# Linear attention and a channel mixer on one core: first half of k requested before lam, first transposes ahead of lam's product, powers of lam after the first mask product

## The chip, the cores and the metric

The kernel runs on 1 core of one Trainium2 chip. The time is device microseconds (us) of that core for one launch. Engines are TensorE (PE; its weight loads are PEld), VectorE (DVE), ScalarE (ACT), GpSimd (POOL) and SyncE (SP). Each takes its instructions in the order in which they stand in its queue. SP and ACT also issue the DMAs here.

## The reference

Inputs q, k, v are (batch 4, heads 8, sequence 768, width 64), lam has one decay per head. The attention is worked in blocks with a running state; its output becomes x, of shape (4, 768, 512), and a mixer follows.

```python
Dmask = np.where(rel >= 0, lam ** rel, 0.0)          # rel = i - j inside a block
intra = (qb @ kb.T * Dmask) @ vb
inter = (qb * lam ** (pos + 1)) @ kv_state
out[block] = intra + inter
kv_state = lam ** block * kv_state + (kb * lam ** (block - 1 - pos)).T @ vb
...
u = x + (x.T @ U @ V).T                              # per batch
result = u + np.maximum(u @ w_ch1, 0) @ w_ch2
```

## The kernel before, in words

The sequence is cut into tiles of 128 positions, 6 per batch, 24 in all; a tile is called s. For a tile, `prep` transposes q and k on TensorE (eight heads, two per transpose, so four transposes each, written to PSUM as `pq` and `pk`) and ScalarE copies them to `qt` and `kt` (L351). `scores` multiplies them into `pss` (L393); `masked` multiplies `pss` by the decay mask on VectorE into `sm` (L402); `intra` multiplies `sm` with v into `px` (L446). `inter` adds `qs` times the running state to the same `px` (L434); `qs` is `qt` times the powers `powq`, made on GpSimd in `scale` (L376). `state` makes the next state `kv` from `ks` (k times `rev`, GpSimd, L365) and v (L411). The first tile of a batch has no state, so tile 0 needs no `qs`; tile 1 is the first that does.

All of the attention part is in an order written out by hand: `manual_schedule` is entered, the opening is written as plain calls, and then the list `pieces` is run from its first entry to its last. The list's order is the order in each engine's queue. After `intra(s)` come `state(s)`, `scores(s+1)`, `inter(s+1)`, `masked(s+1)`, `fade(s+1)`, and `prep(s+2)` stands ahead of `intra(s+1)`.

The opening makes what the tiles need. `lam` (eight numbers) is loaded into `lam_row`, spread over 128 partitions by a small TensorE product `pl` (L662), and copied to `lamb` (L664). From it VectorE makes the mask by eight scans (L302, in `constants`) and the powers `powq` by a memset, two copies and four scans (L308 to L314, in `powers`). `rev` is a column of the mask (L667). `scale_k(0)` then makes tile 0's `ks`.

`keep_busy(n)` issues n products of a zero tile `blank` on TensorE (L336), whose result nobody reads. In PSUM they stand in the buffer that `pq` uses.

Tile 0 is loaded in two halves of four heads each for q and k (`parts(0)` is 2), so that `turn_half(0, 0, ...)` can transpose the first half before the second has landed. The q halves are asked for on SP's DMA queue, the k halves on ACT's; all later loads are on SP's:

```python
nc.scalar.dma_start(out=lam_row[:, 0:H], in_=lam.unsqueeze(0))
load_next("q", nc.sync)
load_next("k", nc.scalar)
```

From 122 us on the mixer's two products (L714, L724, then L847 to L851) fill the rest of the time on TensorE.

In this trace one dummy product shows as two instructions.

Of the kernel before, what the change touches and what calls it, by code (L numbers as in the profile page):

```python
# [14 lines left out]
P = 128  # L15
# [3 lines left out]
def kernel(  # L19
# [28 lines left out]
    nc = tc.nc  # L48

    B, H, S, D = q.shape  # L50
    HP = H // 2
    NT = S // P
    C = H * D
# [34 lines left out]
    def set_ends(t):  # L88
        nc.vector.memset(t[:, 0:1], 1151.0)
        nc.vector.memset(t[:, 1:2], 255.0 * (1 << 23))  # L90
        ends.append(t)
# [153 lines left out]
    def two_banks(name, tag):  # L245
        return psf.tile([P, 2, N], FP32, tag=tag, name=name)

    def one_bank(shape, name, tag):
        return psf.tile(shape, FP32, tag=tag, name=name)
# [11 lines left out]
    def parts(s):  # L261
        return 2 if s == 0 else 1

    def load(name, s, engine):
        b, c = divmod(s, NT)
        t = raw_pool.tile(
            [P, H, D], FP32, tag=f"{name}raw", bufs=4 if name == "k" else 3, name=f"{name}raw"
        )
        source = {"q": q, "k": k, "v": v}[name]
        n = H if name == "v" else H // parts(s)  # L270
        for h in range(0, H, n):
            engine.dma_start(
                out=t[:, h : h + n, :],
                in_=source[b, h : h + n, c * P : (c + 1) * P, :].rearrange("h p d -> p h d"),
            )
        raw[s, name] = t
# [21 lines left out]
    def constants():  # L298
        for a in range(HP):
            for x in range(2):  # L300
                h = 2 * a + x
                nc.vector.tensor_tensor_scan(  # L302
                    mask[:, x, a, :], lamb[:, h : h + 1].broadcast_to([P, P]), ident, 0.0,
                    ALU.mult, ALU.add,
                )

    def powers():
        nc.vector.memset(zeros, 0.0)  # L308
        for x in range(2):
            nc.vector.tensor_copy(  # L310
                out=lamh[x * D : (x + 1) * D, :], in_=lamb[x * D : (x + 1) * D, x::2]
            )
        for a in range(HP):
            nc.vector.tensor_tensor_scan(  # L314
                powq[:, a, :], lamh[:, a : a + 1].broadcast_to([P, P]),
                zeros.broadcast_to([P, P]), 1.0, ALU.mult, ALU.add,
            )
# [13 lines left out]

    def keep_busy(n):

        out = one_bank([P, C], "idle", "pq")
        for i in range(n):
            nc.tensor.matmul(out=out[:, 0:P], lhsT=blank, rhs=blank, start=True, stop=True)  # L336

    qts, kts = {}, {}

    def turn_half(s, a0, name):  # L340

        ts, tag = (qts, ("pq", "pt")) if name == "q" else (kts, ("pk", "pu"))
        if a0 == 0:
            ts[s] = att.tile([P, HP, P], FP32, tag=name + "t", bufs=2, name=name + "t")
        n = HP // parts(s)
        pt = one_bank([P, n, P], "p" + name, tag[a0 > 0])
        for a in range(a0, a0 + n):
            nc.tensor.transpose(  # L348
                out=pt[:, a - a0, :], in_=raw[s, name][:, 2 * a : 2 * a + 2, :], identity=ident
            )  # L350
        nc.scalar.copy(ts[s][:, a0 : a0 + n, :], pt)  # L351

    def prep(s):
        for a0 in range(0, HP, HP // parts(s)):
            for name in "qk":
                turn_half(s, a0, name)
        st[s].update(qt=qts.pop(s), kt=kts.pop(s))
        for name in "qk":
            load_next(name)
# [144 lines left out]
    uhl, ud, turned = {}, {}, {}  # L504
# [39 lines left out]


    pieces = [("prep", 0), ("scale", 0), ("scores", 0), ("inter", 0), ("masked", 0)]
    for s in range(NS):
        b, c = divmod(s, NT)
        done = s - NT - 1
        more = s + 1 < NS  # L550
        step = [("prep", s + 1), ("scale", s + 1)] * more
        step += [("mix", done)] * (0 <= done < NS - NT - 1)
        step += [("low", b - 1)] * (c == 0 and b > 0)
        step += [("low_rows", b - 1)] * (c == 0 and b > 0)
        step += [("intra", s)]
        step += [("next_of_low", b - 1)] * (c == 0 and b > 0)
        step += [("late", s)] * (done < 0) + [("state", s)]
        step += [("next_of_low", b - 1)] * (c == 0 and b > 0)
        step += [("turned", done - 1)] * (done > 0) + [("late", s)] * (done >= 0)
        step += [("next_of_low", b - 1)] * (c == 0 and b > 0)  # L560
        step += [("scores", s + 1)] * more
        step += [("aside", s)] * (done >= 0)
        step += [("inter", s + 1), ("masked", s + 1), ("fade", s + 1)] * more
        step += [("aside", s)] * (done < 0)
        step += [("turn", done)] * (done >= 0 and done // TG < FG)
        pieces += step
    waiting = {name: list(range(NS)) for name in "qkv"}

    def load_next(name, engine=nc.sync):
        if waiting[name]:  # L570
            load(name, waiting[name].pop(0), engine)


    run = {
        "prep": prep, "fade": fade, "scores": scores, "masked": masked, "inter": inter,
        "intra": intra, "state": state,
        "low": low, "low_rows": low_rows, "next_of_low": next_of_low, "mix": mix, "turn": turn,
        "scale": scale, "turned": lambda s: turned.pop(s)(),
    }
    def v_steps():  # L580

# [64 lines left out]
    lam_row = consts.tile([1, H + P], FP32, name="lam_row")  # L646
    blank = x_pool.tile([P, C], FP32, tag="x", name="blank")[:, 0:P]
    nc.vector.memset(blank, 0.0)
    nc.vector.memset(lam_row[:, H:], 1.0)
    set_ends(vp[:, S + C : S + C + 2].bitcast(FP32))  # L650
    nc.scalar.dma_start(out=lam_row[:, 0:H], in_=lam.unsqueeze(0))
    load_next("q", nc.sync)
    load_next("k", nc.scalar)
    for name in "qkvkv":
        load_next(name)
    aside(-1)
    for name in "qkv":
        load_next(name)
    make_identity(nc, ident)
    keep_busy(2)  # L660
    pl = one_bank([P, H], "pl", "pt")
    nc.tensor.matmul(out=pl, lhsT=lam_row[:, H:], rhs=lam_row[:, 0:H], start=True, stop=True)  # L662
    keep_busy(3)
    nc.vector.tensor_copy(out=lamb, in_=pl)  # L664
    constants()
    powers()
    nc.vector.tensor_copy(out=rev, in_=mask[:, :, :, P - 1])  # L667
    scale_k(0)
    run.update(aside=aside, late=on_scalar_late)
# [280 lines left out]
```

## Time and profile before

| | |
|---|---|
| four runs, median | 675.22 us (675.17 to 675.84) |
| the profiled execution | 675.17 us |
| its span (first to last instruction) | 673.2 us |
| TensorE busy, share of span | 666.0 us, 99% |
| VectorE | 498.7 us, 74% |
| ScalarE | 277.2 us, 41% |
| GpSimd | 113.8 us, 17% |
| first dummy product on TensorE | 1.05 us |
| mask product of tile 0 | 8.48 us |
| first `intra` weights of tiles 0 and 1 | 9.77 and 14.06 us |

Times inside a profile count from the start of the span. "busy" of TensorE counts matmuls from start to modelled end, and they overlap, so a busy TensorE is not necessarily at its peak; the start times of its weight loads (PEld) show better when it could go on. A bracket at the end of a line, such as `[1.01 <-PE pss L393]`, says how long the engine had been idle before that instruction and what ended it. `ACTq` and `SPq` are the instructions that issue DMAs.

### The profile page before, as it was taken

Reading aid. Unit: us, or ns where it says so; the run is one execution under the profiler, and the core shown is the slowest. Engines: PE = TensorE matmul, PEld = TensorE weight load, DVE = VectorE, ACT = ScalarE, POOL = GpSimd, SP = SyncE. Lnnn points to the kernel's source line nnn. Section 1 sums busy time; section 2 is a strip of 40 time slices with the busy share of each in tenths; the row PEclk is TensorE's granted clock in tenths of the full one; section 3 lists DMA queues with packets and bytes.
Section 4 is the critical chain, followed back from the end, with each engine's and each line's share of the span. In section 5 each row is a group of like instructions: output and inputs, shape, how many; then the busy total and the mean of one; then the engine's idle time right before and its main releaser. Section 6 shows DMA issues by size and latency. Waiting matters only on the chain.

```text
span 673.2 us, 13173 instructions
## 1 busy us (share of the span) xinstructions
PE 666.0 (99%) x5124; PEld 545.4 (81%) x5124; DVE 498.7 (74%) x879; ACT 277.2 (41%) x513; POOL 113.8 (17%) x92
## 2 busy tenths in 40 slices
PE   9999999999999999999999999999999999999997
PEld 8888888887888888888888888888888888888886
DVE  4689999778999777777797265786686766865864
ACT  4665767455555444444455121332232322322320
POOL 4456767340000000000000000030030200300300
PEclk9999999999999999999999999999999999999999
DMA  8999894264677555565577999854363363453421
GB/s 202 212 238 244 228 219 120 80 220 153 238 265 249 205 203 204 204 204 204 203 275 254 321 317 388 288 184 144 96 209 103 110 203 94 156 157 95 162 89 62
DMA packets 131775, 131.27 MB, mean 195 GB/s; under 512 B 81346, under 2 KB 89794, under 8 KB 131714
## 3 DMA queue, kind: packets, MB, share of 16 engines
q1 hardware_dynamic: 130656, 130.18, 61.1%
q8 instruction: 40, 0.66, 0.4%
q10 hardware_dynamic: 1058, 0.26, 0.2%
q14 instruction: 21, 0.17, 0.1%
HBM read 80.09 MB, written 50.33 MB: 194 GB/s over the span
## 4 chain that ended last, share of the span: by engine, by line
PE 95%; DVE 3%; ACT 1%; issue 0%; DVEq 0%; ACTq 0%
PE pz L714 27%; PE pz L849 13%; PE pz L847 13%; PE pd L724 13%; PE pd L851 13%; PE px L446 3%; PE pss L393 3%; PE put L516 2%; PE pq L348 2%; PE pkv L411 1%; PE px L434 1%; PE pk L348 1%; DVE sm L402 1%; PE pp L461 1%; PE pu L499 1%; PE idle L336 0%
## 5 line engine op out<-in xcount | busy, mean ns | idle before, releaser
L714 PE MATMUL pz<-u_hl,w 128*128 128x512 f32 x768 | 190.5, 397 | 0.0
L714 PEld LDWEIGHTS pz<-u_hl,w 128*128 128x128 f32 x768 | 144.0, 188 | 35.5 <-issue 0.4
L849 PE MATMUL pz<-w_hl,m 128*128 128x512 f32 x384 | 151.1, 396 | 0.0
L847 PE MATMUL pz<-w_hl,m 128*128 128x512 f32 x384 | 150.9, 396 | 0.0
L851 PE MATMUL pd<-w_d,m 128*128 128x512 f32 x384 | 149.5, 396 | 0.0
L830 ACT ACTIVATE m<-mt 128x512 fp32r<-128x512 f32 x96 | 60.6, 632 | 196.0 <-PE pd L851 141.6
L876 POOL TENSOR_TENSOR o<-o,u 128x512 f32<-128x512 f32 x20 | 29.9, 1524 | 447.4 <-DVE o L872 447.4
L831 DVE SCALAR_TENSOR_TENSOR m<-rm,m 128x512 fp32r<-128x512 f32 x96 | 71.4, 746 | 44.9 <-ACT m L830 44.5
L729 DVE SCALAR_TENSOR_TENSOR r<-pd,r 128x512 f32<-128x512 f32 x96 | 61.8, 686 | 54.0 <-ACT r L720 43.5
L724 PE MATMUL pd<-u_d,w 128*128 128x512 f32 x384 | 98.6, 397 | 0.0
L720 ACT ACTIVATE r<-pz 128x512 f32<-128x512 f32 x96 | 52.2, 596 | 93.8 <-PE pz L714 93.1
L849 PEld LDWEIGHTS pz<-w_hl,m 128*128 128x128 f32 x384 | 72.3, 188 | 17.7
L847 PEld LDWEIGHTS pz<-w_hl,m 128*128 128x128 f32 x384 | 72.3, 188 | 17.6
L851 PEld LDWEIGHTS pd<-w_d,m 128*128 128x128 f32 x384 | 72.3, 188 | 17.6
L724 PEld LDWEIGHTS pd<-u_d,w 128*128 128x128 f32 x384 | 72.1, 188 | 17.3
L829 DVE TENSOR_SCALAR mt<-rm 128x512 uint32<-128x512 uint32 x96 | 46.2, 482 | 35.0 <-DMA rm<-r_d 34.8
L832 DVE SCALAR_TENSOR_TENSOR m<-m 128x512 fp32r<-128x512 f32 x96 | 69.1, 721 | 0.9
L402 DVE TENSOR_TENSOR sm<-pss,mask 128x512 f32<-128x512 f32 x48 | 30.8, 684 | 6.0 <-PE pss L393 5.9
L205 ACT CAST w<-wt 128x512 fp32r<-128x512 f32 x32 | 19.9, 620 | 30.6 <-DVE wt L202 23.4
L446 PEld LDWEIGHTS px<-vraw,sm 128*64 128x64 f32 x768 | 24.7, 137 | 6.6 <-DVE sm L402 3.0
L376 POOL TENSOR_TENSOR qs<-qt,powq 128x512 f32<-128x512 f32 x20 | 25.9, 1296 | 22.8 <-ACT qt L351 22.8
L446 PE MATMUL px<-vraw,sm 128*64 128x64 f32 x768 | 28.4, 226 | 0.9 <-DVE sm L402 0.7
(85 smaller groups left out, 684.4 us busy)
## 6 DMA issues: line engine op xcount, KB each, us to landing
r_d<-r SPq DMA_DIRECT2D x96, 256.0 KB, 2.3
rm<-r_d SPq DMA_DIRECT2D x96, 256.0 KB, 2.7
words<-in_moe_w_ch_dram SPq DMA_DIRECT2D x30, 512.0 KB, 4.3
w_d<-w SPq DMA_DIRECT2D x16, 768.0 KB, 3.3
w_hl<-w_d SPq DMA_DIRECT2D x16, 512.0 KB, 6.4
vraw<-in_v_dram SPq DMA_DIRECT2D x24, 256.0 KB, 4.3
u_d<-x_nat SPq DMA_DIRECT2D x24, 256.0 KB, 3.1
u<-u_d SPq DMA_DIRECT2D x24, 256.0 KB, 4.0
```

The source lines that it names most:

```text
L446: nc.tensor.matmul(out=px[half[t], x, a, :], lhsT=sm[:, x, a, half[t]], rhs=vr[:, 2 * a + x, :], start=(first and a == 0), stop=(a == HP - 1),
L714: nc.tensor.matmul(out=acc[g][0], lhsT=w[:, n, ct, :], rhs=uhl[g][:, n, ct, :], start=(ct == 0 and n == 0), stop=(ct == CT - 1 and n == 1),)
L720: nc.scalar.mul(rs[g], acc[g][0], 4096.0 + 1.0)
L724: nc.tensor.matmul(out=acc[g][1], lhsT=w[:, 2, ct, :], rhs=ud[g][:, ct, :], start=(ct == 0), stop=(ct == CT - 1),)
L729: nc.vector.scalar_tensor_tensor(rs[g], acc[g][1], 4096.0, rs[g], ALU.mult, ALU.add)
L829: nc.vector.tensor_scalar(t.bitcast(U32), r.bitcast(U32), HI, None, ALU.bitwise_and)
L830: nc.scalar.activation(out=m[:, 0], in_=t, func=AF.Relu)
L831: nc.vector.scalar_tensor_tensor(m[:, 1], r, 0.0, hi, ALU.max, ALU.subtract)
L832: nc.vector.scalar_tensor_tensor(m[:, 2], hi, E, low, ALU.mult, ALU.subtract)
L847: nc.tensor.matmul(out=pz, lhsT=m[:, 0, cols], rhs=hl[:, 0], start=first, stop=False)
L849: nc.tensor.matmul(out=pz, lhsT=m[:, 1, cols], rhs=hl[:, 1], start=False, stop=end)
L851: nc.tensor.matmul(out=pd, lhsT=m[:, 2, cols], rhs=dd, start=first, stop=end)
```

## The change

Four edits, all in the opening:

- On ACT's DMA queue the two halves of k for tile 0 are asked for ahead of lam.
- Four dummy products instead of two come first on TensorE, then the transposes of the first halves of q and k, then lam's product, one dummy instead of three, and the transposes of the second halves. `prep(0)` no longer transposes; it only hands on `qt` and `kt`.
- The dummies write to the buffer of `px` and `pl` to that of `pss`, since `pq` and `pt` are now in use at that point.
- `powers` leaves the opening and becomes a piece of its own, right after `masked(0)`.

```diff
     def keep_busy(n):
-        out = one_bank([P, C], "idle", "pq")
+        out = two_banks("idle", "px")[:, 0, 0:P]
         for i in range(n):
-            nc.tensor.matmul(out=out[:, 0:P], lhsT=blank, rhs=blank, start=True, stop=True)
+            nc.tensor.matmul(out=out, lhsT=blank, rhs=blank, start=True, stop=True)
...
     def prep(s):
-        for a0 in range(0, HP, HP // parts(s)):
+        for a0 in range(0, HP, HP // parts(s)) if s > 0 else ():
             for name in "qk":
                 turn_half(s, a0, name)
...
     pieces = [("prep", 0), ("scale", 0), ("scores", 0), ("inter", 0), ("masked", 0)]
+    pieces += [("powers", 0)]
...
-        "scale": scale, "turned": lambda s: turned.pop(s)(),
+        "scale": scale, "powers": lambda s: powers(), "turned": lambda s: turned.pop(s)(),
...
-    nc.scalar.dma_start(out=lam_row[:, 0:H], in_=lam.unsqueeze(0))
     load_next("q", nc.sync)
     load_next("k", nc.scalar)
+    nc.scalar.dma_start(out=lam_row[:, 0:H], in_=lam.unsqueeze(0))
...
     make_identity(nc, ident)
-    keep_busy(2)
-    pl = one_bank([P, H], "pl", "pt")
+    keep_busy(4)
+    for name in "qk":
+        turn_half(0, 0, name)
+    pl = two_banks("pl", "pss")[:, 0, 0:H]
     nc.tensor.matmul(out=pl, lhsT=lam_row[:, H:], rhs=lam_row[:, 0:H], start=True, stop=True)
-    keep_busy(3)
+    keep_busy(1)
+    for name in "qk":
+        turn_half(0, HP // 2, name)
     nc.vector.tensor_copy(out=lamb, in_=pl)
     constants()
-    powers()
     nc.vector.tensor_copy(out=rev, in_=mask[:, :, :, P - 1])
```

## The prediction

> **What bounds the kernel now.** I read the page first, then the chain of waits for the first 30 us, then the timeline of the first 16 us, then the DMA issues of that stretch. The page gives TensorE 666.0 of the 673.2 us of the span, and its chain is 95% TensorE, so whatever the change does it must do to the moment at which TensorE comes into its steady run. The chain's beginning (start, length, what; all us):
>
> ```profile
> 1.05 1.23 PE idle L336 x4
> 2.28 0.52 PE pl L662 x2
> 2.80 1.58 PE idle L336 x6
> 4.38 0.10 issue
> 4.48 0.66 PE pq L348 x2
> ...
> 6.42 2.01 PE pss L393 x16
> ...
> 9.85 1.08 PE px L446 x32
> ...
> 14.13 1.08 PE px L446 x32
> ...
> 18.42 1.08 PE px L446 x32
> ...
> 28.55 1.11 PE pss L393 x16
> 29.67 0.02 issue
> 29.69 0.69 DVE sm L402
> ```
>
> Nothing on it is a wait for a load. From the second tile on, a tile costs 4.29 us (9.85, 14.13, 18.42), all TensorE. At 29.69 the chain passes to VectorE, and again through the release of its operand: the mask product started when the scores ended. So a delay before 10 us is handed on in full; I see no slack that would swallow it, and take it one to one (the other end, that the VectorE stretch after 29.69 swallows all, has no row for it).
>
> The timeline of the same stretch shows who feeds that chain:
>
> ```profile
> 0.73 0.52 ACTq L651 DMA_DIRECT2D lam_row<-in_lam_dram  x1
> 1.29 0.97 ACTq L272 DMA_DIRECT2D kraw<-in_k_dram  x2
> 2.84 0.17 DVE L664 COPY lamb<-pl 128x8 f32<-128x8 f32 x1 [1.70 <-PE pl L662]
> 3.11 2.63 DVE L302 TENSOR_TENSOR_SCAN mask<-lamb,ident 128x128 f32<-128x128 f32 x8
> 6.04 1.37 DVE L314 TENSOR_TENSOR_SCAN powq<-small 128x128 f32<-128x128 f32 x4
> 8.48 1.29 DVE L402 TENSOR_TENSOR sm<-pss,mask 128x512 f32<-128x512 f32 x2 [1.01 <-PE pss L393]
> 10.11 1.28 POOL L376 TENSOR_TENSOR qs<-qt,powq 128x512 f32<-128x512 f32 x1 [0.47 <-ACT qt L351]
> 12.41 0.56 PEld L434 LDWEIGHTS px<-kv,qs 64*64 64x64 f32 x32
> ```
>
> VectorE had masks, powers and `rev` ready at 7.48 and then waited 1.01 us for the scores. The powers stood in that shadow and cost nothing. They are wanted by `qs` of tile 1 on GpSimd (10.11), and that by `inter` of tile 1 on TensorE (12.41).
>
> The DMA issues of the first 13 us, KB and us from issue to landing:
>
> ```profile
> qraw<-in_q_dram SPq DMA_DIRECT2D x2, 128.0 KB, 3.0
> kraw<-in_k_dram ACTq DMA_DIRECT2D x2, 128.0 KB, 3.5
> ```
>
> The single issues are 2.4 and 3.7 us for q's halves, 3.4 and 3.6 for k's. lam, a few bytes, was issued at 0.73 and its product's weights went in at 2.21: at most 1.48 us.
>
> **The change, part by part.** I call T the time at which lam's product `pl` starts on TensorE (2.21 before), and M the start of tile 0's mask product (8.48 before).
>
> *Instructions.* None is added or removed: five dummy products before, four and one after, the same transposes and scans. Only order and waits differ. The dummies leave q's PSUM buffer, so q's first transpose need no longer wait for the last dummy to drain. Weights stood idle 0.37 us there; at most that is saved, and I book nothing, since below lam is later.
>
> *ACT's DMA queue.* k's halves are issued 0.56 us earlier (1.29 to 0.73), lam 0.94 later: 0.73 + 0.97 = 1.70. SyncE's queue is untouched. k's first half lands at 0.73 + 3.4 = 4.1 (from 3.1, if it goes as fast as q's first half, 2.4). When lam lands has two ends. If it is as quick as before, 1.70 + 1.48 = 3.18. If it lands with the half of k issued just ahead of it: that half, issued at 1.16, lands at 4.66 by the mean 3.5, and 0.1 more for the start of the product makes 4.75. At the far end, by k's second half as it landed before (1.74 + 3.6 = 5.34) plus the 0.22 us that weights stood idle ahead of `pl`, T is 5.5. I take T = 4.75, because that neighbour on the same queue is the nearest row. The Trainium skill ("DMA: Bandwidth & Descriptors", section on queues, rings and completion order) says that descriptors of one queue are consumed in ring order on each DMA engine. That speaks against this edit, since lam's few bytes would stand behind 256 KB of k; by that rule T is the 4.75, without it the lower bound below. No row of this trace has lam behind a big transfer.
>
> *First halves turned ahead of `pl`.* TensorE runs in order, so `pl` also waits for both first halves: q's is there at 3.14, its two transposes take 0.43, k's 0.43. With k at 4.1, T is at least 4.55; with k as fast as q, 4.0. So T lies between 4.0 and 5.5, and lam's landing decides by a little. Before, `pl` was out of the way at 2.73; now a wait for lam holds the last dummy, the second halves, the scores and everything after.
>
> *From T to M on TensorE, at the rates of these rows:* `pl` to the next dummy 0.52 (2.21 to 2.73), one dummy 0.43, q's second half 0.43, k's 0.43: scores start at T + 1.81. First halves were copied long before, so the old wait of 0.33 for ScalarE goes. Scores to mask product took 2.13 (6.35 to 8.48). Their second half needs k's late copy: transposes to copy's end took 0.84 + 0.41, so about T + 2.7, against T + 2.67 when the first half is through; I add 0.1. M = T + 1.81 + 2.13 + 0.1 = T + 4.04 = 8.79, which is 0.31 later than before.
>
> *From T to M on VectorE:* `pl` to `lamb` 0.63, to the scans 0.27, eight scans 2.63, `rev` 0.15: ready at T + 3.68, 0.36 before M. That part is covered; if the scores got faster by more than 0.36 the scans would bound. GpSimd's `ks` of tile 0 moves from 7.56 to about 8.5 and ends at 9.6; `state` wants it at M + 2.2 = 11.0, so it costs nothing.
>
> *Powers behind the mask product.* The memset, two copies and four scans take from 5.67 to 7.41, 1.74 us. Now they start at M + 1.29 and end at M + 3.03. `qs` of tile 1 starts 0.08 later (as `ks` did after `rev`), runs 1.28 and ends at M + 4.39; 0.1 to reach TensorE gives M + 4.48. Before, `inter` started at 12.41 = M + 3.93. TensorE therefore waits 0.55 us, and behind it in its queue stand the transposes of tile 2 and `intra` of tile 1. The mask product of tile 1, at M + 4.05, is not delayed, and `kv`'s copy (11.44 = M + 2.96) loses under 0.1. `ks` of tile 2 follows `qs` on GpSimd and is needed a tile later. The shadow that hid the powers is gone and nothing takes its place. Ends: 0.0 if TensorE is later anyway by as much, 0.7 if the scans are slowed beside GpSimd's `ks`.
>
> *Sum:* 0.31 + 0.55 = +0.86. The profiled execution took 675.17, of which 1.97 lie outside its span; it is the fastest of four, 0.05 below the median 675.22. 675.17 + 0.86 = 676.0. A measurement of this kernel can tell about 0.2%, 1.35 us, from no change, so this is inside it.
>
> **The rivals.**
>
> *lam far behind (slower).* One DMA engine late with k's second half holds lam too, T = 5.5: M = 9.54, 1.06 late, plus 0.55 is +1.61: 676.8. For it: the second half did land as late as 5.34. Against: lam needs one engine, not the latest of all. It counts as slower from T = 5.24.
>
> *The clock rises later (slower).* The granted clock's row reads 1.00 throughout, but TensorE's own rows show a slow start: in the scores 16 weight loads took 1.79 us at tile 0 and 0.97 at tile 1, and the change lies at about 9.1, 8.0 us after the first product. After the change TensorE stands idle between its four dummies (done near 3) and T. If eight unbroken microseconds are needed and the count starts anew at T = 4.75, the rise comes at 12.8. From `intra` of tile 0 at M + 1.29 = 10.1 on, TensorE would lose half of 2.7 us, 1.35; 0.55 of that lies in the wait for `qs`. So +0.86 + 0.8 = +1.66: 676.8. At most, the whole 8.0 us later, half of 7.0 less 0.55: +3.8. Against: before, the rise came while scores ran, and after it scores run in the same microseconds (6.6 to 8.7). The page "TensorE: Matmul & The Clock Gate" (Part 1) has a free-running activity window of 3.4 us; by its figure a missed window would put the rise at about 12.5, some 1.5 us in all, an estimate from that page.
>
> *Everything early (not slower).* k lands as q did and lam as before: T = 4.0, M = 8.04, 0.44 early, and the powers' 0.55 is swallowed by later waits: 674.7, still inside the bound. To be faster by 1.35 the mask product would have to start near 7.1 even without the powers' cost, and `pl` by 3.1, before q's half has landed and been turned.
>
> *It does not do what it says:* the order of the instructions is as described on each engine, so this has no chance of its own.
>
> **How the numbers follow.** Main case 0.50, of which 0.04 lies above 676.5; lam far behind 0.22; clock later 0.18; everything early 0.07; something faster that these rows do not show 0.03. Faster 0.03, same 0.46 + 0.07 = 0.53, slower 0.04 + 0.22 + 0.18 = 0.44. The main case's own range is 675.4 to 676.5 (T from 4.3 to 5.2). The wide range reaches into the early case and past the two slower ones: 675.1 to 677.3.
>
> **What would show it.** Right: `pl` near 4.75 with idle before it put down to issue or a DMA; `lamb` at 5.4; the mask product of tile 0 at 8.8 with only a short wait; `powq` from 10.1 to 11.8; `qs` at 11.9; a wait of weights ahead of `inter` near 13.2 that was not there before; `intra` of tile 1 at 14.9 instead of 14.06 and 4.29 per tile from there. Wrong: `pl` below 4 or above 5.3, tile 0's weight loads still slow beyond 10 us, `inter` without a wait, or a shift at 20 us that is not there at the end.

## The result and the profile after

| | before | after |
|---|---|---|
| median, runs | 676.14 us, 62 | 676.81 us, 41 |
| lowest and highest | 674.27, 678.02 | 676.43, 677.30 |
| the profiled execution, its span | 675.17, 673.16 | 676.72, 674.94 |
| `pl` on TensorE | 2.21 | 4.66 |
| mask product of tile 0 | 8.48 | 8.88 |
| `powq` ready | 7.41 | 12.16 |
| `inter`, then `intra` of tile 1 | 12.41, 14.06 | 13.63, 15.28 |

The ratio of the times is 1.0011, 95% interval 1.0006 to 1.0016: slower by 0.67 us by the medians, inside the 0.2% that was called no change. Two things in this table are not what the forecast assumed. The two profiled executions differ by 1.55 us, more than twice the medians. And the kernel before spreads over 3.75 us, the changed one over 0.87. What moved was the kernel before: in the order of the record the first 31 of its 62 runs have the median 675.53 and the last 31 676.70, while the changed kernel's first 20 and last 21 have 676.83 and 676.75.

The chain of waits of the changed kernel, from its start (start, length, what; us):

```profile
0.74 2.77 DMA qraw<-in_q_dram
...
4.73 0.52 PE pl L665 x2
...
6.83 2.01 PE pss L393 x16
8.84 1.04 PE pq L348 x4
9.88 0.85 PE pk L348 x4
10.73 1.37 PE px L446 x32
12.10 0.47 PE pkv L411 x16
12.57 1.09 PE pss L393 x16
13.66 0.66 PE px L434 x32
...
15.35 1.08 PE px L446 x32
...
19.64 1.08 PE px L446 x32
```

It now begins with a load, as the first transposes have nothing ahead of them but four dummies, and from 3.64 to 15.35 it stays on TensorE. `intra` of tile 1 starts 1.22 us later than before (15.35 against 14.13), and from there a tile again takes 4.29 us. The timeline has the two steps in which the 1.22 arise:

```profile
1.85 0.61 ACTq L654 DMA_DIRECT2D lam_row<-in_lam_dram  x1
4.66 0.50 PEld L665 LDWEIGHTS pl<-lam_row 1*128 1x128 f32 x2 [0.33 <-issue]
5.29 0.17 DVE L669 COPY lamb<-pl 128x8 f32<-128x8 f32 x1 [4.15 <-PE pl L665]
8.88 1.29 DVE L402 TENSOR_TENSOR sm<-pss,mask 128x512 f32<-128x512 f32 x2 [0.48 <-PE pss L393]
10.10 0.48 DVE L310 COPY small<-lamb 64x4 f32<-64x4 f32 x1
10.79 1.37 DVE L314 TENSOR_TENSOR_SCAN powq<-small 128x128 f32<-128x128 f32 x4
12.31 1.27 POOL L376 TENSOR_TENSOR qs<-qt,powq 128x512 f32<-128x512 f32 x1 [1.75 <-DVE powq L314]
12.50 0.97 PEld L393 LDWEIGHTS pss<-qt,kt 64*128 64x128 f32 x16
13.63 0.56 PEld L434 LDWEIGHTS px<-kv,qs 64*64 64x64 f32 x32 [0.16 <-POOL qs L376]
```

The mask product starts 0.40 late. From it to `inter` of tile 1 went 3.93 us before and 4.75 now, 0.82 more. Two paths were later by nearly the same. One is powers, then `qs`, which ended at 13.58; GpSimd waited 1.75 us for `powq`, where before it had waited 0.47 and for `qt`. The other is TensorE itself: its weight loads were slow until 11.3 instead of 9.2, so in the chain `pk` took 0.85 for 0.44 and `intra` of tile 0 1.37 for 1.08. Its last weights ahead of `inter` ended at 13.47; with the 0.12 that stands there in the profiles without a wait for `qs`, `inter` would have started at 13.59, 0.78 late, without any wait for the powers. lam's load, issued at 1.85 behind k, landed at 4.48 by the trace.

At the start of the mixer there is a third step, which the forecast did not have. The weight loads there, the kernel before and then the changed one:

```profile
120.99 1.10 PEld L446 LDWEIGHTS px<-vraw,sm 128*64 128x64 f32 x32 [0.24 <-issue]
122.15 0.19 PEld L714 LDWEIGHTS pz<-u_hl,w 128*128 128x128 f32 x1
...
122.21 1.10 PEld L446 LDWEIGHTS px<-vraw,sm 128*64 128x64 f32 x32 [0.24 <-issue]
124.13 0.75 PEld L718 LDWEIGHTS pz<-u_hl,w 128*128 128x128 f32 x4 [0.82 <-ACT x_nat L451]
```

Before, `pz` followed `intra` at once. Now it waits until ScalarE has copied `px` out, and the distance grows from 1.22 to 1.77, which is that of the spans (1.78).

### The profile page after: what moved, and what is told of

Same layout as the page of the kernel before. It is cut to its first block, busy times and chain, and to the rows that moved or that the text cites. A ratio compares the mean times of both kernels' runs of the same rounds, so it can differ in the third digit from the quotient of the medians.

```text
span 674.9 us, 13172 instructions
## 1 busy us (share of the span) xinstructions
PE 666.7 (99%) x5124; PEld 545.9 (81%) x5124; DVE 499.4 (74%) x879; ACT 277.3 (41%) x513; POOL 113.8 (17%) x92
## 4 chain that ended last, share of the span: by engine, by line
PE 94%; DVE 3%; ACT 1%; DMA 1%; issue 0%; SPq 0%; DVEq 0%; ACTq 0%
PE pz L718 27%; PE pz L853 13%; PE pz L851 13%; PE pd L728 13%; PE pd L855 13%; PE pss L393 3%; PE px L446 3%; PE put L516 2%; PE pq L348 1%; PE pkv L411 1%; PE pk L348 1%; PE px L434 1%; DVE sm L402 1%; PE pp L461 1%; PE pu L499 1%; DMA u_d<-x_nat 0%
```

## The experiments

All distances in this table are to the first profile of the kernel before, in us, worked out from the starts of the same TensorE weight loads in both traces. "mixer" is the fifth weight load of the first `pz`. The ratios and intervals beside the runs are over all runs of both kernels and need not be the quotient of the medians. The kernel before was run beside each group of experiments: on chip 13 for the four from "PSUM order kept" to "lam first" (675.3), on chip 7 for the others (676.01 and 676.15).

| profile of | `pl` | mask product | `inter` tile 1 | distance at tile 1 | tile 23 | mixer | end of span |
|---|---|---|---|---|---|---|---|
| the change | 4.66 | 8.88 | 13.63 | 1.22 | 1.22 | 1.77 | 1.78 |
| the change, again | 4.71 | 8.94 | 13.69 | 1.28 | 1.29 | 1.86 | 1.86 |
| PSUM order kept | 4.67 | 8.90 | 13.64 | 1.23 | 1.22 | 1.22 | 1.20 |
| powers alone | 2.21 | 9.03 | 14.12 | 1.71 | 1.71 | 1.71 | 1.72 |
| powers in the opening | 4.79 | 9.97 | 13.83 | 1.42 | 1.41 | 1.98 | 1.99 |
| lam first | 5.35 | 9.58 | 14.33 | 1.92 | 1.92 | 2.49 | 2.52 |
| k ahead alone | 4.56 | 10.00 | 13.87 | 1.45 | 1.46 | 1.46 | 1.46 |
| `ks` of tile 1 behind `qs` | 4.74 | 8.97 | 13.40 | 0.98 | 0.99 | 0.99 | 0.97 |
| lam on GpSimd | 4.80 | 11.06 | 14.89 | 2.48 | 2.47 | 2.48 | 2.61 |
| lam on ScalarE, first halves on SyncE | 3.05 | 9.30 | 13.14 | 0.73 | 1.42 | 1.42 | 1.42 |
| lam between q's halves | 3.87 | 8.42 | 12.49 | 0.07 | 0.36 | 0.36 | 0.34 |
| before, second profile | 2.20 | 7.79 | 11.65 | -0.56 | 0.85 | 0.85 | 1.07 |
| before, third profile | 2.21 | 8.48 | 12.35 | -0.06 | 0.01 | 0.01 | 0.12 |

**PSUM order kept.** In the change the dummies and `pl` are the first to take the buffers `px` and `pss`, so by the code the PSUM pool hands out its banks in another order than before, and the pool of the mixer is laid over the same banks. The run takes the buffers in the old order ahead of everything:

```diff
+    for tag in ("pq", "pt", "pk", "pu"):
+        one_bank([P, C], "hold", tag)
+    for tag in ("pss", "px"):
+        two_banks("hold", tag)
     keep_busy(4)
```

> The changed kernel, with its PSUM buffers given out in the order of the kernel before. Theory (three terms: mask product of tile 0 later by 0.4 us, wait for qs of tile 1 by 0.8, and 0.55 at the start of the mixer because its first PSUM bank is now the one that ScalarE reads last): the opening stays as in the changed kernel, the first pz weights follow intra with no wait for ScalarE, and the span is 0.55 us shorter: about 676.3 against 676.8. Rival (all of the difference comes from a clock that rose 2.1 us later in the changed kernel's profile, the buffers do not matter): 676.8, as the changed kernel.

The opening is that of the change to 0.02 us, and the wait at the mixer is gone:

```profile
123.37 0.19 PEld L722 LDWEIGHTS pz<-u_hl,w 128*128 128x128 f32 x1
```

The distance stays at 1.22 and the span is 0.58 shorter. The median of ten runs is 676.18 (676.04 to 676.77); all 41 runs of the change are at 676.43 or above, nine of these ten below 676.5. Against the kernel before beside it (675.3) the ratio is 1.0013 (1.0003 to 1.0022), no lower than the change's 1.0011, as the kernel before is lower there than its median of 676.14. The record does not name the chips of the 41 runs, so it is the trace, more than the medians, that shows the 0.55.

**Powers alone.** The kernel before with `("powers", 0)` behind `masked(0)` and nothing else.

```diff
     constants()
-    powers()
...
+    pieces += [("powers", 0)]
```

> The kernel before with one edit, powers behind the first mask product. Theory: mask product of tile 0 stays at 8.5, powq ends at 11.5 to 11.8, qs ends near 13, and inter of tile 1 starts near 13.2 instead of 12.41, 0.7 to 0.8 later if the clock has risen by 10 us; no wait at the start of the mixer. Median 0.3 to 0.8 above the kernel before, and less spread, since TensorE waits there whatever its clock did. Rival (the powers find cover elsewhere): inter at 12.4, no difference.

676.19 against 675.3, ratio 1.0006 (0.9995 to 1.0016). The profile does not isolate the wait. k's second half landed at 6.23 in it instead of 5.34, so the mask product started 0.55 late, and TensorE's rows were slow until 12.3, so TensorE came to `inter` at 14.12 while `qs` had ended at 13.40. The path through the powers is as expected (ready 2.96 us after the mask product's start, since GpSimd had ended its `ks` by then), but the run is inconclusive about its cost.

**Powers in the opening.** The change with the powers ahead of `rev` again.

```diff
     constants()
+    powers()
...
-    pieces += [("powers", 0)]
```

> The changed kernel with powers back in the opening, ahead of rev. Theory: pl still starts near 4.7, so VectorE is ready only at about pl + 5.4 = 10.1 and the mask product of tile 0 starts there instead of 8.88; no wait for qs, inter of tile 1 at 10.1 + 3.93 = 14.0 instead of 13.63; 0.4 us slower than the changed kernel, 677.2. Rival (the moved powers are the whole loss): 0.8 us faster than the changed kernel, 676.0.

677.38 (ratio 1.0034, 1.0020 to 1.0047), 0.57 above the change. The mask product starts at 9.97, bound by VectorE, and no wait for `qs` is left; `inter` is 0.20 later than in the change. So with lam this late the powers are better behind the mask product: moving them pays back part of what the first two cost.

**lam first.** The change with lam's load again ahead of k's.

```diff
+    nc.scalar.dma_start(out=lam_row[:, 0:H], in_=lam.unsqueeze(0))
     load_next("q", nc.sync)
     load_next("k", nc.scalar)
-    nc.scalar.dma_start(out=lam_row[:, 0:H], in_=lam.unsqueeze(0))
```

> The changed kernel with lam again ahead of k on ScalarE's DMA queue. Theory (pl stands behind the later of lam and the first half of k): lam lands before 2, but k's first half again near 4.7, so pl starts at 5.2 to 5.3 instead of 4.66; mask product of tile 0 at 9.4, all 0.5 us later than the changed kernel: 677.3. Rival (lam's late landing alone holds pl): pl near 4.0, mask product at 8.3, 0.5 us faster than the changed kernel.

677.49 (1.0038, 1.0024 to 1.0053). k's first half landed at 4.69, `pl` moved to 5.35, and all else followed by 0.70. With the transposes ahead of `pl`, the first two edits belong together. Here TensorE's rows had turned fast before 10, and the wait for `qs` stands open in the weight loads:

```profile
5.35 0.50 PEld L665 LDWEIGHTS pl<-lam_row 1*128 1x128 f32 x2 [0.33 <-issue]
14.33 0.56 PEld L434 LDWEIGHTS px<-kv,qs 64*64 64x64 f32 x32 [1.00 <-POOL qs L376]
```

From the mask product to `inter` went 4.75 us, as in the change, and TensorE by itself would have been there after 3.81: 0.94 is what the moved powers cost where TensorE is fast. In the change itself the same wait showed as 0.16 only, because TensorE was slow until about 11 there and arrived late anyway.

**k ahead alone.** The kernel before with lam's load behind k's and nothing else.

```diff
-    nc.scalar.dma_start(out=lam_row[:, 0:H], in_=lam.unsqueeze(0))
     load_next("q", nc.sync)
     load_next("k", nc.scalar)
+    nc.scalar.dma_start(out=lam_row[:, 0:H], in_=lam.unsqueeze(0))
```

> The kernel before with one edit, k's halves issued ahead of lam on ScalarE's DMA queue; pl still first on TensorE with three dummies and all transposes behind it. Theory (lam waits behind k in the queue): pl starts near 4.6, the transposes near 6.4, scores near 8.3, mask product of tile 0 near 10.4; with powers still ahead of it VectorE is ready at 10.1, so both agree; about 1.9 us later than the kernel before if the clock rises alike, less where it has risen by then: 676.6 to 677.5. Rival (a few bytes slip past the queue): pl by 3.4, no difference.

677.36 (1.0021, 1.0011 to 1.0030). `pl` at 4.56, the mask product at 10.00, when the scores ended, with VectorE ready 0.17 earlier: both close together, as expected. The rival that a few bytes slip past the queue falls.

**lam on GpSimd's queue.** lam by GpSimd's DMA, `pl` ahead of the transposes, half of the powers behind `rev` and ahead of the mask product, the PSUM order kept. Against the change:

```diff
-    nc.scalar.dma_start(out=lam_row[:, 0:H], in_=lam.unsqueeze(0))
+    nc.gpsimd.dma_start(out=lam_row[:, 0:H], in_=lam.unsqueeze(0))
...
     keep_busy(4)
+    pl = ...; nc.tensor.matmul(out=pl, ...)
     for name in "qk":
         turn_half(0, 0, name)
-    pl = ...; nc.tensor.matmul(out=pl, ...)
-    keep_busy(1)
...
     nc.vector.tensor_copy(out=rev, in_=mask[:, :, :, P - 1])
+    powers()            # memset, copies, scans 0 and 1
...
-        "powers": lambda s: powers(), ...
+        "powers": lambda s: powers(HP // 2), ...    # scans 2 and 3
```

> The changed kernel with lam on GpSimd's DMA queue, pl ahead of the transposes with no dummy behind it, two of the four power scans (and the copies) ahead of the mask product and two behind it, and the PSUM buffers in the old order. Theory: pl near 2.9, scores near 5.3 as k's second half lands at 4.7, mask product of tile 0 near 7.6, powq ready at 9.7, qs ends at 11.0, inter of tile 1 near 11.5 without a wait: 0.9 us earlier than the kernel before at the same clock, about 674.9 against its 675.3 to 676.1. Rival (the opening only moves the wait to VectorE or to a clock that has not risen): inter near 12.4, no difference to the kernel before.

677.95 (1.0031, 1.0017 to 1.0045): wrong twice. lam, issued at 1.24, landed at 4.70. And two scans took 2.30 us beside GpSimd's `ks`, as the timeline shows, where two scans without it took 0.72:

```profile
8.63 2.22 POOL L366 TENSOR_TENSOR ks<-kraw,small 128x512 f32<-128x512 f32 x2 [6.09 <-DVE small L675]
8.84 2.30 DVE L315 TENSOR_TENSOR_SCAN powq<-small 128x128 f32<-128x128 f32 x2
12.24 0.72 DVE L315 TENSOR_TENSOR_SCAN powq<-small 128x128 f32<-128x128 f32 x2
```

**lam on ScalarE's queue, first halves of q and k on SyncE's.** Otherwise as the run just told.

```diff
-    nc.gpsimd.dma_start(out=lam_row[:, 0:H], in_=lam.unsqueeze(0))
-    load_next("q", nc.sync)
-    load_next("k", nc.scalar)
+    nc.scalar.dma_start(out=lam_row[:, 0:H], in_=lam.unsqueeze(0))
+    load_next("q", (nc.sync, nc.scalar))    # first half, second half
+    load_next("k", (nc.sync, nc.scalar))
```

> As the run with lam on GpSimd's queue, but lam first on ScalarE's DMA queue, with the second halves of q and k behind it there, and the first halves of q and k on SyncE's. Theory: pl near 2.9 (behind four dummies), k's first half lands near 4.0, the second halves near 5, scores near 5.6, mask product near 7.9, inter of tile 1 near 11.8: 0.6 us earlier than the kernel before at the same clock. Rival: as there, no difference.

677.07 (1.0017, 1.0007 to 1.0027). `pl` came at 3.05, but k's first half not before 5.1, and the scans again took 2.29 beside `ks`, so the mask product started at 9.30 and not near 7.9: a miss as well.

**`ks` of tile 1 behind `qs` of tile 1.** Built on the run with the PSUM order kept; `scale(0)` no longer makes `ks` of tile 1, `scale(1)` makes it behind `qs`.

```diff
     def scale(s):
...
-        if s + 1 < NS:
-            scale_k(s + 1)
+        for n in () if s == 0 else (1, 2) if s == 1 else (s + 1,):
+            if n < NS:
+                scale_k(n)
...
```

> The changed kernel with its PSUM buffers in the old order and, on GpSimd, ks of tile 1 moved from ahead of qs of tile 1 to behind it. Theory (the powers' first copy took 0.48 instead of 0.15 us because GpSimd's ks of tile 1 ran until 10.55): with nothing on GpSimd after 9.6 that copy takes 0.16, powq is ready 0.3 us earlier at 11.85, qs starts at 12.0 and inter of tile 1 at 13.3 instead of 13.64; the total is 0.3 us below the run with the PSUM buffers kept, about 675.9. Rival (the copy is slow behind the mask product for its own reason): copy at 0.48, same total.

```profile
10.19 0.16 DVE L310 COPY small<-lamb 64x4 f32<-64x4 f32 x1
10.56 1.37 DVE L314 TENSOR_TENSOR_SCAN powq<-small 128x128 f32<-128x128 f32 x4
```

The copy takes 0.16 instead of 0.48, from the mask product to `inter` go 4.43 us instead of 4.74, and the span is 0.23 shorter. `qs` ended at 13.34, just as TensorE came for it, so what is left of the delay there, 4.43 for 3.93, is TensorE's own slow start (its rows turned fast at about 10.5). 676.03, ratio 0.9998 (0.9988 to 1.0008).

**lam between q's halves.** The run with lam on GpSimd's queue, with three edits: lam on SyncE's queue behind q's first half, half of the powers ahead of `rev` so that GpSimd starts behind them, and `ks` of tile 1 behind `qs` as in the run before this one.

```diff
             engine.dma_start(out=t[:, h : h + n, :], ...)
+            if (s, name, h) == (0, "q", 0):
+                engine.dma_start(out=lam_row[:, 0:H], in_=lam.unsqueeze(0))
...
-    nc.gpsimd.dma_start(out=lam_row[:, 0:H], in_=lam.unsqueeze(0))
...
+    powers()
     nc.vector.tensor_copy(out=rev, in_=mask[:, :, :, P - 1])
-    powers()
...
```

> lam on SyncE's DMA queue between q's two halves, k's halves first on ScalarE's queue, pl behind four dummies and ahead of all transposes, half of the powers ahead of the mask product and ahead of rev, ks of tile 1 behind qs of tile 1, PSUM buffers in the old order. Theory: lam lands at 3.1 to 3.4, pl near 3.4, scores near 5.7, mask product of tile 0 near 8.1, inter of tile 1 near 12.0 without a wait, 0.4 us ahead of the first profile of the kernel before. If openings are handed on in full: 0.4 us below it. If, as in the second profile of the kernel before, the loads of v then come too late for a tile near 30 us, the gain is gone by there and the total is the same as before, 675.3 to 676.2.

675.54 against 676.15 for the kernel before beside it, ratio 0.9992 (0.9980 to 1.0004). lam landed at 3.76, not by 3.4, and `inter` came at 12.49 and not 12.0. By these runs it cannot be told from the kernel before. Its median is 1.27 below the change's, and none of its ten runs (675.29 to 676.57) reaches the change's median.

**The two kernels once more.** The kernel before again, the change again, and the kernel before a third time, with no edit.

> The kernel before once more, for a second profile and the spread of its times. Theory (its opening follows the moment at which TensorE's rows turn fast, which differs from run to run): if the rows turn fast later than the 9.1 of the first profile, intra of tile 1 and the end are later by up to half of that; times spread over 2 us or more, where the changed kernel spread over 0.9. Rival (the spread comes from elsewhere): the same start times in the opening with another total.

> The changed kernel once more, for a second profile. Theory (its late opening leaves the loads time, so that no tile waits for one): intra of tile 5 starts 1.2 us later than in the first profile of the kernel before and the distance stays 1.2 up to tile 23 and 1.8 behind it; v of tile 5 lands 2 us or more ahead of its use. Rival: distances that change from tile to tile as in the second profile of the kernel before.

> The kernel before, a third profile. Theory (its spread comes from single late loads behind an early opening, and from the moment TensorE's rows turn fast): if the total is above 675.5, a tile's intra after tile 1 starts late against the first profile, with a load landing at that moment; if not, all distances are those of the opening. Rival: the total moves with the opening alone.

The second profile of the kernel before (676.24) opens 0.56 us earlier than the first, since TensorE's rows turned fast at about 6.9, and ends 1.07 later. The 0.56 is gone at tile 5, where the chain of waits runs through a load:

```profile
24.98 6.29 DMA vraw<-in_v_dram
31.28 0.14 issue
31.41 1.15 PE px L446 x32
```

v of tile 5 was there 1.56 us ahead of its use in the first profile and 0.10 here. Further steps of 0.35, 0.45 and 0.22, and one of 0.20 back, follow up to the mixer and behind it. In the third profile (675.29) the distances are small throughout. In the change v of tiles 4 and 5 was there 3.1 and 3.9 us ahead of its use, 2.5 and 3.1 in its second profile, and the distance does not move from tile 1 to tile 23. For the same `v` of tile 4 the kernel before had 0.25, 0.52 and 0.31 us.

## Why the prediction was right, and where not

The direction, "no change, rather slower", and the size of the medians' difference (0.67 against +0.86) came out. The second is luck: from profile to profile the sum was 0.69 too small, and the kernel before has its median 0.97 above the profile that served as base. The changed kernel's 676.81 lies above the main case's own range (675.4 to 676.5), at the 676.8 that both slower rivals named; it counts as no change because the kernel before came out at 676.14. Of the signs of being wrong two came: tile 0's weight loads were slow beyond 10 us, and the shift at 20 us (1.22) was not the one at the end (1.78).

*lam behind k, T.* The number is right, 4.66 and 4.71 against 4.75; what decided it is not. lam's issue took its place at 1.85, 1.12 later than before, as k's two took 1.09 and not 0.97 us (the prediction's "0.94 later" is 0.97 by its own row). lam came with its neighbour on the queue: issued at 1.85, landed at 4.48, against 4.72 for k's second half and 3.79 for its first. In the four runs in which `pl` stood waiting for lam it started 0.10 to 0.11 after the landing, so lam alone would have let it go at 4.59. The chain has the first half of q and the transposes instead. q's half landed at 3.51, where the forecast kept 3.14, the last transposing weights ended at 4.33, and 0.33 later `pl` began. That 0.33 is not a wait for lam: the same stood there in the run with lam first, where lam had been there since 1.92. "Everything early" and "a few bytes slip past" fall; "lam far behind" did not come either.

*T to M.* Right: 4.22 for 4.04 in the change, so M 0.40 late instead of 0.31. The scores started at T + 2.10 instead of 1.81, as the wait of 0.33 ahead of them that the prediction took away was still there, and the 0.1 for their second half was not needed. VectorE was ready 0.48 before M, cover that the forecast put at 0.36.

*Powers behind the mask product.* The path through the powers was as described and came 0.82 late instead of 0.55. That TensorE waits for it by that much is not shown: in the change's first profile TensorE was 0.78 late by itself and the powers added 0.04, in its second 0.49 and 0.33. The term had TensorE at the pace of the kernel before, and its lower end, 0.0 where TensorE is later anyway by as much, is near what the first profile shows. Where TensorE was fast early (lam first) the wait was 0.94. The prediction priced the scans beside GpSimd's `ks` as its upper end of 0.7; what was slowed was the copy ahead of them, by 0.32, and moving `ks` away took 0.31 off the step. The Trainium skill ("SBUF — State Buffer", section "Who interferes with whom") says that a VectorE copy can block fully on a running GpSimd instruction when it runs in a mode that takes both ports, that an instruction with two SBUF inputs contends with one that reads SBUF, and that one with at most one SBUF input, outside those modes, does not. The rows agree: the copy ended with `ks`, the scans of the GpSimd run took three times as long, and the mask product (one input in PSUM) kept its 0.69 a piece beside `ks`.

*A term that was not there.* The PSUM order costs 0.55 at the mixer, 115 us behind the edits. It was told in the diff as a change of buffer names, and I costed it only where the dummies stand.

*The base.* 675.17 was taken as the time of the kernel before. Its median over 62 runs is 0.97 above that, so the profile that the sum was made on lies near the lower end of its spread. The changed kernel's profile is 0.09 below its median. So the sum from profile to profile should have been 1.55 and was forecast as 0.86, and the medians differ by 0.67 because the kernel before is about one microsecond slower in many runs than in its first four (675.22). Against those four the change is 1.59 slower, against its last 31 runs (676.70) 0.1. Part of this may go with the chip: beside the experiments the median was 675.3 on chip 13 and 676.01 and 676.15 on chip 7. What moved it was not found.

*"A delay is handed on in full".* Right for a long delay: in the nine profiles that open 0.9 us or more late the distance at tile 1 is that at tile 23 within 0.02 us. Wrong for a gain and for a short delay: the second profile of the kernel before gave 0.56 back, and more, and the runs that opened 0.07 and 0.73 late were 0.36 and 1.42 late at tile 23. Those two did not lose it to v: the first step came at tile 3, whose v had been there for more than 1 us, inside the weight loads of its `inter`, where the profile shows nothing that they wait for.

*The spread.* With the opening 1.2 us later, the loads of v have 2.5 us or more in hand instead of 0.3. That this is why the change's times spread less is not shown, and other runs speak against it: five of the experiments (powers alone, powers in the opening, k ahead alone, `ks` behind `qs`, lam on GpSimd) had 3.6 us or more in hand for tiles 4 and 5, and their runs spread over 1.27 to 1.78 us. The spread goes better with another thing: in the three kernels in which `inter` of tile 1 waits for `qs` it is 0.87 (41 runs), 0.73 (10, PSUM order kept) and 0.83 (5, lam first), in the seven others 1.27 to 2.59. Such a wait would take up the differences in when TensorE turns fast. That is a reading of one or two profiles a kernel and, in the others, of 5 to 10 runs; no run tests it.

*The clock later.* It did rise later in both profiles of the change (at 11.3 and 10.7 by TensorE's rows) than in those of the kernel before (9.2, 6.9, 8.4), and cost nothing on top: the distance at tile 1 is 1.22 and 1.28, since the wait for `qs` covered it. It was not free by itself: with the powers in time the same rows would have cost 0.78 and 0.49, and in the run with `ks` behind `qs`, where no wait for `qs` is left, they cost 0.50. The rival's price of 0.8 on top was wrong, as the rise came at 11.3 and not 12.8 and `qs` 0.27 later than assumed. The page "TensorE: Matmul & The Clock Gate" of the Trainium skill (Part 1) has the activity window free-running, so that the moment differs between runs of one kernel. The three profiles of the kernel before agree in that; their moments lie 5.8 to 8.2 us after the first product and 2.3 us apart, where the page gives around 4 us of sustained activity and 500 ns either way.

## What to carry to other kernels

A wait at the head of an in-order queue is only free while something else ends later, and a delay is only worth what the next limit leaves of it: here lam's product came 2.45 us later and cost 0.40, and the moved powers, 0.94 where TensorE was fast, added 0.04 and 0.33 where it was late itself. When a buffer gets its first user in a new place, look at the order in which the pool hands out its memory, and at who lies on the same bank a hundred microseconds on. And take more than one profile of the kernel before, and at more than one time: a base from the lower end of the spread puts its distance to the median into every forecast, and an opening that is early can lose its lead to a load that is not there yet (0.56 us, gone at tile 5).

## What the runs showed of the hardware

- In these runs a load of a few bytes was about as late as the big loads issued around it, on whichever queue: issue to landing took 1.2 us when it was the first of all (0.73 to 1.91), 2.6 behind two halves of k on ScalarE's queue, 2.5 behind one half of q on SyncE's (1.23 to 3.76), and 3.5 alone on GpSimd's (1.24 to 4.70).
- VectorE's scans with both inputs in SBUF took 2.30 us a pair beside a GpSimd multiplication and 0.72 without; a small copy 0.48 instead of 0.16.
- q's first half, the first load on SyncE's queue, landed at 3.40 to 3.59 in the eight profiles in which k's was issued beside it at 0.73, and at 2.88 to 3.15 in the six in which lam was issued there first.
- A load can hang on one late completion: of the 16 of v's load for tile 5 in the second profile of the kernel before, 15 had come by 29.34 and the last came at 31.28, just ahead of `intra` of that tile (31.38).
- TensorE's rows turned from some 0.21 to 0.11 us per 128-column weight load at times between 6.9 and 12.3 us of the span, in kernels that all start TensorE at 1.05. In three profiles of the kernel before the times were 9.2, 6.9 and 8.4.
